# Placement of pools on 64-byte multiples, an even spread of attention visits, and another order of the last segments, in one kernel of attention and expert layer

## Chip, cores and metric

The kernel runs on one NeuronCore of a Trainium2 chip. The metric is the device time of one execution in microseconds (us). The engines are named as in the profile: PE is TensorE's matmul, PEld its weight load, DVE is VectorE, ACT is ScalarE, POOL is GpSimd, SP is SyncE, whose queue issues most DMA transfers.

## What is computed

For 8 batches and 8 heads (576 positions, head width 64) a sparse attention: heads 0 to 3 see the 32 positions behind and with the query (local), heads 4 to 7 those at the same residue modulo 32 (strided). The 4608 x 512 result is put through a layer with 2048 features and a squared ReLU.

```python
mask_local = (rel >= 0) & (rel < stride)
mask_strided = (rel >= 0) & (pos[None, :] % stride == pos[:, None] % stride)
scores = np.where(masks[None, :, :, :], scores, -1000000000.0)
attn = np.exp(scores - np.max(scores, axis=-1, keepdims=True))
attn = attn / (np.sum(attn, axis=-1, keepdims=True) + 1e-09)
x = np.matmul(attn, v).transpose(0, 2, 1, 3).reshape(4608, 512)
h = np.maximum(x @ w_in, 0.0)
return h * h @ w_out
```

## The kernel before

**Chunks.** The 24 segments of 192 positions (three of a batch) are taken in the order of `SEGS` (line 86). Chunks 0 to 3 have 384 of these columns, chunks 4 to 9 have 512. For each chunk the expert layer runs over 16 feature tiles j. An up block of j (`up`, line 687) is 12 products `h<-x,w`: all operands are split into a high and a low part in float32r, so each of four slices of `x` takes three products. `features` (line 692) then makes relu and square on ACT, the high part `gh` on ACT and the low part `gl` on DVE. A down block (`down`, line 720) is three products `y<-w,g` for each 128 columns, with `g` as the stationary and `w_out` as the moving operand. In chunks 2 and 3 the loop (line 1000) takes four j as a group of four stages k: two j up, two j up, two j down, two j down. From chunk 4 on (line 1026) each j is one stage: up of j, down of j - 1.

**Local attention.** Heads are worked by `Head` (line 285), for groups of one or two segments; a head has one or two parts of two windows. A visit (line 422) is four small products placed between two blocks: two outputs `o<-px,vx` of part i - 3 and two scores `s<-kx,qx` of part i. Its steps follow on the other engines: `cast` (`kx`, `qx`: ACT and POOL), `soft` (exponentials on ACT), `flip` (transposes into `p_t` on DVE), `turn` (`px`: ACT and DVE), `values` (`vx`), and loads on SP's queue. In chunks 4 to 8 and in chunk 3 `event` (line 948) gives the steps of a visit, in chunk 2 `four` (line 801). Steps are issued behind the features of a certain j (`behind_features`, line 968). Results go through `st` to the local part of `x` (`xlh`, `xll`, line 412), for the chunk that holds their columns.

**Strided attention.** This runs on POOL and DVE without PE: a `Range` (line 536) is a run of up to 12 blocks of 32 queries of one batch. It loads `qs`, `ks`, `vs` (or one short tile `qkvs`), clears `sc` on POOL (line 568), makes products on POOL (`pq`, line 576) that DVE sums (line 581), takes a softmax, makes products with the values (`pp`, line 609) that DVE sums (line 613), transposes, and writes the strided part of `x`: `xsh` on ACT (line 627) and `xsl` on POOL (line 631). `strided(c + 1)` is handed out during chunk c by `spread` (line 922), by a planner's cost of each range. The instructions are put in order by a scheduler, so ranges can run ahead of the chunk that hands them out, as far as buffers allow.

**Pools.** `hold` and `drop` (lines 157 to 162) stack pools from the left and the right end of the memory: on the left `strided` (five wide tiles or q, k, v, then `sc` of 864 bytes, then two `prod`), `features` (`gh`, `gl`) and `x1`; on the right `raw`, `x0`, later `tail`. `x0` and `x1` hold `x` of even and odd chunks. In the program's placement all tiles of `features`, `x0`, `x1` and `raw` begin 32 bytes past a multiple of 64, as `prod` does; the weights and the tiles of `lpool` and `lraw` (`kx`, `qx`, `px`, `vx`) begin at a multiple of 64. The pairs of chunk 1 take their `qk` once from `lraw` and once from `raw` (line 769).

Of the kernel before, what the change touches and what calls it, by code (L numbers as in the profile page):

```python
# [7 lines left out]
F32 = mybir.dt.float32  # L8
# [14 lines left out]
P = 128  # L23
TC = 384
WP = 512
NFT = DF // P
# [46 lines left out]
"""  # L73

GROUP = 4
TURN, SOFT = 0, 2
NSHARE = 10


# [1 line left out]
def f32(ap):  # L81
# [4 lines left out]
SEGS = (  # L86
    (0, 0), (1, 0), (2, 0), (3, 0), (4, 0), (6, 1), (0, 1), (0, 2),
    (7, 0), (5, 0), (5, 1), (5, 2), (1, 1), (1, 2), (7, 1), (7, 2),
    (2, 1), (2, 2), (3, 1), (3, 2), (6, 0), (6, 2), (4, 1), (4, 2),
)  # L90
SEG = TC // 2
SI = SEG // STR
# [1 line left out]
NEARLY, LATE = 4, 512  # L94
SIZES = [TC] * NEARLY + [LATE] * ((NT - NEARLY * TC) // LATE)
NCHUNK = len(SIZES)
# [46 lines left out]
def attn_moe(ctx: ExitStack, tc, qk_l, v_l, qk_d, v_d, qk_p, v_p, f_s, q_s, k_s, v_s, w_in, w_out, masks, eye, out):  # L143
# [11 lines left out]
    held, reach = {}, [0]  # L155

    def hold(name, side="left"):
        held[name] = tc.alloc_tile_pool(name=name, bufs=1, side=side, reuse_waits="tile")

    def drop(*names):  # L160
        for name in names:
            held.pop(name).release()

    for name in ("strided", "features", "x1"):
        hold(name)
    for name in ("raw", "x0"):
        hold(name, "right")

    def wide(shape, nm, dt=F32, query=False):

        tag, bufs = ("s3", 5) if reach[0] <= NEARLY else ("q", 2) if query else ("kv", 3)
        return held["strided"].tile(shape, dt, name=nm, tag=tag, bufs=bufs)
# [10 lines left out]
    turn = iter(range(10000))  # L183
# [235 lines left out]
    heads = [Head(n) for n in range(HL * (len(GROUPS) - NPLAIN))]  # L419
    parts = [(h, a) for h in heads for a in range(0, h.nw, 2)]  # L420

    def visit(o=None, s=None, banks=(4, 3)):


        jobs = [parts[n][0].outputs(parts[n][1], banks[0]) for n in ([] if o is None else [o])]
        jobs += [parts[n][0].scores(parts[n][1], banks[1]) for n in ([] if s is None else [s])]
        for two in zip(*(products for products, _ in jobs)):
            for make in two:
                chain(make)
        behind_pe(*(rest for _, rest in jobs))  # L430

    def behind_pe(*steps):
        with tc.issue_after(last["pe"].ins):
            for step in steps:
                step()
# [244 lines left out]
    def every(j):  # L680
        parts = [(kt, w, s) for kt in range(4) for w, s in ((0, "h"), (0, "l"), (1, "h"))]
        if j < 2:

            parts.sort(key=lambda i: i[0] < 2 and i[2] == "l")
        return parts
# [112 lines left out]
        }  # L798
        return table[g - 8]

    def four(q):


        n = len(heads)
        h = q - 2
        some = lambda i, what: [(what, i)] if 0 <= i < n else []
        v = lambda i: [("v", i - 3 if 0 <= i - 3 < 2 * n else None, i if i < 2 * n else None)] if i - 3 < 2 * n else []
        return (
            (v(2 * h) + some(h - 1, "values"), some(h - 1, "turn") + some(h + 1, "load"), TURN),
            ([], [], None),  # L810
            (v(2 * h + 1), some(h + 1, "cast") + some(h, "soft") + some(h, "flip"), SOFT),
            ([], [], None),
        )

    def do(steps):
        for what, *k in steps:
            if what == "s":
                visit(None, k[0])
            elif what == "S":
                visit(None, k[0], banks=(4, 4))  # L820
            elif what == "O":
                visit(k[0], None, banks=(3, 3))
            elif what == "v":
                visit(*k)
            else:
                h = heads[k[0]]
                early = [h.values] if what == "turn" and not hasattr(h, "vx") else []
                step = getattr(h, what)
                args = (4,) if what == "turn" else ()
                with ExitStack() as st:  # L830
                    for i in begin_end.values() if h.c == NPLAIN else ():
                        st.enter_context(tc.issue_after(i.ins))
                    behind_pe(*early, lambda: step(*args))
# [88 lines left out]
    def spread(c, j):  # L922

        if c + 1 == NCHUNK:
            return
        if j == 0:
            st = strided(c + 1)
            if c == 1:
                st = behind(begin_end, st)
            cost = sum(2 * sum(range(i0 + 1, i1 + 1)) + 10 for _, i0, i1, _ in ranges(c + 1))  # L930
            work.update(st=st, cost=cost, ds=0)
        while work["ds"] < (j + 1) / SPREAD * work["cost"]:
            k = next(work["st"], "end")
            if k == "end":
                break
            work["ds"] += k
        if j == NFT - 1:
            run(work["st"])

    def stage(part, steps):  # L940

        for step in steps:
            with tc.issue_after(last["pe"].ins):
                for i, *tiles in step:
                    last["mm"] = part(*divmod(i, NFT), *tiles)
            last["pe"] = last["mm"]

    def event(i):


        o, n = i - 3, len(parts)
        visits, steps = [("v", o if o < n else None, i if i < n else None)], []
        if o + 1 < n and parts[o + 1][1] == 0:
            h = parts[o + 1][0].n
            visits.append(("values", h))
            steps.append(("turn", h))
            if NSHARE < h + 1 < len(heads):
                steps.append(("load_v", h + 1))
        if i < n and parts[i][1] == parts[i][0].nw - 2:
            h = parts[i][0].n  # L960
            if h + 1 < len(heads):
                steps.append(("cast", h + 1))
            if h + 2 < len(heads):
                steps.append(("load_qk", h + 2))
            steps += [("soft", h), ("flip", h)]
        return visits, steps

    def behind_features(i, steps):
        with ExitStack() as st:
            for k in feats[divmod(i, NFT)]:  # L970
                st.enter_context(tc.issue_after(k.ins))
            do(steps)

    def land(c):

        for h, st, hp, *place in [e for e in carried if e[3] == c]:
            h.split(st, hp, *place)
        carried[:] = [e for e in carried if e[3] != c]

    turns = iter(range(2 * NSHARE, len(parts) + 3))  # L980

    with tc.issue_after(last["v"].ins):
        for t in p_t:
# [16 lines left out]
    for s in range(2 * NFT, NEARLY * NFT, GROUP):  # L1000
        c, j = divmod(s, NFT)
        slots = range(s, s + GROUP)
        if j == 0:
            reach[0] = c + 1
        if s == (NEARLY - 1) * NFT:
            drop("x0", "raw")
            hold("x0", "right")
            hold("tail", "right")
            do([("load_qk", NSHARE + 1)])
        for k in range(GROUP):  # L1010
            if c + 1 < NEARLY:
                visits, steps, slot = four(s // GROUP)[k]
            else:
                visits, steps = event(next(turns)) if k < 3 else ([], [])
                slot = k
            do(visits)
            mine = [(i,) for i in slots[k % 2 * 2 : k % 2 * 2 + 2]]
            if k < 2:
                stage(up, [mine])
            else:  # L1020
                stage(down, [[m for m in mine if m != (NEARLY * NFT - 1,)]])
            if slot is not None:
                behind_features(s + slot, steps)
            spread(c, j + k)

    for c in range(NEARLY, NCHUNK):
        reach[0] = c + 1
        for j in range(NFT):
            i = c * NFT + j
            visits = steps = []  # L1030
            if c + 1 < NCHUNK and (j % 2 == 0 if (c - NEARLY) % 3 == 1 else j % 4 != 3):
                n = next(turns, None)
                if n is not None:
                    visits, steps = event(n)
            do(visits)
            if i == NEARLY * NFT:
                stage(products, [[(i, every(0), True, True)]])
                stage(down, [[(i - 1,)]])
                drop("x1", "features", "strided")
                hold("strided")  # L1040
                hold("x1")
                hold("features")
                features(c, j)
            else:
                stage(up, [[(i,)]])
                if i < NS - 2:
                    stage(down, [[(i - 1,)]])
            if j == 0:
                land(c + 1)
            behind_features(i - 1, steps)  # L1050
            spread(c, j)
    i = NS - 3
# [2 lines left out]
    stage(down, [[(i + k, (t,)) for k in (1, 2) for t in range(3)]])  # L1055
    y_rest += [psum(i, f"y_rest{i}") for i in range(2)]
    stage(down, [[(i + k, (3,), h) for k in (1, 2)] for h in range(2)])
    drop("tail", "x0", "features", "x1", "strided")


_NAMES = ["qk_l", "v_l", "qk_d", "v_d", "qk_p", "v_p", "f_s", "q_s", "k_s", "v_s", "w_in", "w_out", "masks", "eye"]
# [72 lines left out]
```

## Time and profile before

| | us |
|---|---|
| median of 3 runs | 904.2 |
| lowest and highest | 901.33 and 904.57 |
| profiled execution | 904.06 |
| its span, first to last instruction | 902.3 |
| PE busy in the span | 878.2 (97%) |
| DVE, ACT, POOL busy | 650.1, 555.1, 670.0 |

A matmul's row shows its own duration with its latency, about 0.4 us for 512 columns; consecutive products overlap, so the distance of two starts tells the pace. The granted clock of PE is given as a share of its upper level. "Idle" is time in which an engine did nothing before the instruction shown, with the releaser behind an arrow.

### The profile page before, as it was taken

What the parts mean: (1) busy time and instruction counts of PE and PEld (TensorE: products, weight loads), DVE (VectorE), ACT (ScalarE), POOL (GpSimd) and SP (SyncE); (2) the same over time, 40 slices, a digit from 0 to 9 for tenths busy, and PEclk for the clock granted to TensorE, in tenths of its full rate; (3) what the DMA queues carried; (4) which work ended last, traced back from release to release, by engine and by line L of the source; (5) the groups of instructions that cost most, each with busy time, mean ns of one, the idle gap of its engine ahead of it and who ended that gap; (6) DMA issues with size and microseconds to landing.
All of it is one profiled execution on the core that took longest, in us unless ns stands there. A gap on an engine that the chain in (4) does not pass through costs nothing.

```text
span 902.3 us, 13966 instructions
## 1 busy us (share of the span) xinstructions
PE 878.2 (97%) x4364; PEld 737.4 (82%) x4364; DVE 650.1 (72%) x1940; ACT 555.1 (62%) x1436; POOL 670.0 (74%) x781
## 2 busy tenths in 40 slices
PE   9999999999988899998999999999999999989998
PEld 8988989989877778887888888878887888868886
DVE  7998988868877788877777778878787777541111
ACT  7997776755766576665655666676676654333332
POOL 5998778978885979897888987988887889750000
PEclk9999999999999999999999999999999999999999
DMA  9954513110204122131400221134022410000001
GB/s 356 360 196 156 165 60 111 66 45 21 81 26 143 47 67 84 43 92 52 141 25 24 72 69 33 47 95 138 27 79 86 142 32 1 1 12 36 1 1 47
DMA packets 30682, 73.97 MB, mean 82 GB/s; under 512 B 3408, under 2 KB 13264, under 8 KB 29072
## 3 DMA queue, kind: packets, MB, share of 16 engines
q1 hardware_dynamic: 30176, 72.69, 24.2%
q8 instruction: 34, 0.56, 0.2%
q10 hardware_dynamic: 432, 0.39, 0.1%
q14 instruction: 40, 0.33, 0.1%
HBM read 63.64 MB, written 9.44 MB: 81 GB/s over the span
## 4 chain that ended last, share of the span: by engine, by line
PE 80%; DVE 6%; POOL 5%; ACT 5%; issue 2%; DMA 0%; POOLq 0%
PE y L735 39%; PE h L677 37%; POOL pp L609 2%; PE s L335 2%; POOL pq L576 2%; PE o L394 1%; DVE p_t L368 1%; DVE sc L581 1%; DVE gl L705 1%; POOL qx L324 1%; DVE qs L613 1%; ACT e L484 1%; ACT raw L229 1%; POOL kx L322 1%; ACT e L355 1%
## 5 line engine op out<-in xcount | busy, mean ns | idle before, releaser
L735 PE MATMUL y<-w,gh 128*128 128x512 f32 x1148 | 380.6, 396 | 0.0
L735 PEld LDWEIGHTS y<-w,gh 128*128 128x128 f32 x1148 | 215.6, 188 | 51.5
L735 PE MATMUL y<-w,gl 128*128 128x512 f32 x574 | 226.9, 395 | 0.0
L576 POOL TENSOR_TENSOR pq<-ks,qs 128x512 f32<-128x512 f32 (+3 forms) x198 | 202.2, 1041 | 24.2 <-DVE sc L581 18.9
L677 PE MATMUL h<-xsh,w 128*128 128x512 f32 (+1 forms) x640 | 210.9, 375 | 1.6 <-ACT xsh L627 1.6
L609 POOL TENSOR_TENSOR pp<-vs,sc 128x448 f32<-128x448 f32 (+11 forms) x198 | 194.0, 1004 | 22.5 <-DVE qs L613 20.1
L677 PE MATMUL h<-xlh,w 128*128 128x512 f32 (+1 forms) x640 | 206.8, 377 | 0.3 <-DVE gl L705 0.3
L694 ACT ACTIVATE h<-h 128x512 f32<-128x512 f32 (+1 forms) x144 | 78.6, 546 | 160.5 <-PE h L677 159.3
L705 DVE TENSOR_TENSOR gl<-h,gh 128x512 fp32r<-128x512 f32 (+1 forms) x160 | 101.1, 632 | 95.9 <-ACT gh L701 94.6
L581 DVE TENSOR_REDUCE sc<-pq 128x8 f32<-128x512 f32 (+4 forms) x228 | 118.8, 532 | 35.0 <-POOL pq L576 31.5
L677 PEld LDWEIGHTS h<-xsh,w 128*128 128x128 f32 x640 | 120.9, 191 | 19.5 <-ACT xsh L627 2.0
L677 PEld LDWEIGHTS h<-xlh,w 128*128 128x128 f32 x640 | 120.3, 191 | 16.6 <-DVE gl L705 0.6
L613 DVE TENSOR_REDUCE qs<-pp 128x64 f32<-128x448 f32 (+12 forms) x198 | 109.5, 557 | 33.9 <-POOL pp L609 31.5
L735 PEld LDWEIGHTS y<-w,gl 128*128 128x128 f32 x574 | 107.8, 188 | 25.5 <-DVE gl L705 0.2
L677 PE MATMUL h<-xsl,w 128*128 128x512 f32 (+1 forms) x320 | 117.6, 376 | 1.4 <-POOL xsl L631 1.4
L677 PE MATMUL h<-xll,w 128*128 128x512 f32 (+1 forms) x320 | 115.1, 377 | 0.0
L368 DVE STREAM_TRANSPOSE p_t<-e 32x128 f32<-32x128 f32 (+1 forms) x288 | 80.4, 279 | 20.7 <-ACT e L360 16.7
L701 ACT CAST gh<-h 128x512 fp32r<-128x512 f32 (+1 forms) x160 | 86.8, 543 | 12.1 <-PE y L735 6.6
L695 ACT ACTIVATE h<-h 128x512 f32<-128x512 f32 (+1 forms) x144 | 78.6, 546 | 3.4
L355 ACT ACTIVATE e<-e,nm 96x128 f32<-96x128 f32 x160 | 62.9, 395 | 19.3 <-DVE nm L343 18.7
L677 PEld LDWEIGHTS h<-xsl,w 128*128 128x128 f32 x320 | 60.8, 191 | 10.6 <-POOL xsl L631 1.7
L677 PEld LDWEIGHTS h<-xll,w 128*128 128x128 f32 x320 | 60.8, 191 | 6.7
(110 smaller groups left out, 1106.6 us busy)
## 6 DMA issues: line engine op xcount, KB each, us to landing
y<-ysb SPq DMA_DIRECT2D x35, 256.0 KB, 2.2
vs<-v_s SPq DMA_DIRECT2D x13, 576.0 KB, 3.7
raw<-w_in SPq DMA_DIRECT2D x7, 1024.0 KB, 10.3
qk<-qk_l SPq DMA_DIRECT2D x16, 416.0 KB, 3.2
qk<-qk_l SPq DMA_DIRECT2D x16, 400.0 KB, 3.1
raw<-w_out SPq DMA_DIRECT2D x5, 1024.0 KB, 11.9
ks<-k_s SPq DMA_DIRECT2D x8, 576.0 KB, 3.7
v<-v_l SPq DMA_DIRECT2D x32, 128.0 KB, 2.0
```

What stands on the lines that cost most here:

```text
L355: nc.scalar.activation(ev[:, w], ev[:, w], AF.Exp, bias=self.nmax[:QC, w : w + 1], scale=-1.0, accum_out=ssum[:QC, w, :1])
L368: nc.vector.transpose(out=pt[STR * k : STR * (k + 1), :, STR * r : STR * (r + 1)], in_=self.ev[STR * r : STR * (r + 1), :, STR * k : STR * ...
L576: nc.gpsimd.tensor_mul(pv, self.k[:, a : a + m, :], self.q[:, i - self.i0 : i - self.i0 + 1, :].broadcast_to([P, m, D]))
L581: nc.vector.tensor_reduce(out=self.sc[:, i - self.i0, a : a + m], in_=self.prods.pop(("m", n)), op=ALU.add, axis=AX.X)
L609: nc.gpsimd.tensor_mul(pv, self.v[:, a : a + nd, :m], self.sc[:, il : il + 1, :m].broadcast_to([P, nd, m]))
L613: nc.vector.tensor_reduce(out=self.q[:, i - self.i0, a : a + nd], in_=self.prods.pop(("p", n)), op=ALU.add, axis=AX.X)
L677: done = nc.tensor.matmul(h_ps[c, j][:, : SIZES[c]], wi[p][w][:, wsl], x["ls"[kt // 2], s][:, kt % 2, :], start=fresh and n == 0, stop=ful ...
L694: nc.scalar.activation(g, g, AF.Relu)
L695: nc.scalar.activation(g, g, AF.Square)
L701: return nc.scalar.copy(gh, g)
L705: return nc.vector.tensor_sub(gl, g, f32(gh))
L735: done = nc.tensor.matmul(into, g[:, t * P : (t + 1) * P], wo[p][w][:, wsl], start=j == fresh and k == 0, stop=shut and k == 2)
```

## The change

Pools: on the left the order becomes `features`, `x1`, `strided`, so that the `sc` of 864 bytes lies behind what PE reads; on the right a pool `edge` with one tile of 32 bytes is put first. Visits: `four`, `TURN` and `SOFT` go, and chunks 2 and 3 take their visits from `event` as the later chunks do. A table `VISITS` gives the number of visits of each chunk (10 and 10 for chunks 2 and 3, before 8 and 12; the others as before), and `turn_at` spreads them over the 16 j. `event` gets the loads of the first ten heads; the separate `load_qk` at the start of chunk 3 goes. Segments: the last four places of `SEGS` are (4,1), (4,2), (6,0), (6,2) instead of (6,0), (6,2), (4,1), (4,2).

```diff
-    (2, 1), (2, 2), (3, 1), (3, 2), (6, 0), (6, 2), (4, 1), (4, 2),
+    (2, 1), (2, 2), (3, 1), (3, 2), (4, 1), (4, 2), (6, 0), (6, 2),
...
-    for name in ("strided", "features", "x1"):
+    for name in ("features", "x1", "strided"):
         hold(name)
-    for name in ("raw", "x0"):
+    for name in ("edge", "raw", "x0"):
         hold(name, "right")
+    held["edge"].tile([P, 8], F32, name="edge", tag="edge")
...
+        if i < n and parts[i][1] == 0 and parts[i][0].n < NSHARE:
+            steps.append(("load", parts[i][0].n + 1))
         if i < n and parts[i][1] == parts[i][0].nw - 2:
             h = parts[i][0].n
             if h + 1 < len(heads):
                 steps.append(("cast", h + 1))
-            if h + 2 < len(heads):
+            if NSHARE < h + 2 < len(heads):
                 steps.append(("load_qk", h + 2))
...
-    turns = iter(range(2 * NSHARE, len(parts) + 3))
+    VISITS = {2: 10, 3: 10, 4: 12, 5: 8, 6: 12, 7: 12, 8: 8, 9: 0}
+    turns = iter(range(12, len(parts) + 3))
+
+    def turn_at(c, j):
+
+        n = VISITS[c]
+        return next(turns, None) if j * n // NFT != (j - 1) * n // NFT else None
...
-            do([("load_qk", NSHARE + 1)])
         for k in range(GROUP):
-            if c + 1 < NEARLY:
-                visits, steps, slot = four(s // GROUP)[k]
-            else:
-                visits, steps = event(next(turns)) if k < 3 else ([], [])
-                slot = k
+            n = turn_at(c, j + k)
+            visits, steps = ([], []) if n is None else event(n)
             do(visits)
...
-            if slot is not None:
-                behind_features(s + slot, steps)
+            behind_features(s + k, steps)
...
-            visits = steps = []
-            if c + 1 < NCHUNK and (j % 2 == 0 if (c - NEARLY) % 3 == 1 else j % 4 != 3):
-                n = next(turns, None)
-                if n is not None:
-                    visits, steps = event(n)
+            n = turn_at(c, j)
+            visits, steps = ([], []) if n is None else event(n)
...
-                drop("x1", "features", "strided")
-                hold("strided")
-                hold("x1")
-                hold("features")
+                drop("strided", "x1", "features")
+                for name in ("features", "x1", "strided"):
+                    hold(name)
```

## Rows read from the trace of the kernel before

**Rows 1.** The page, part 1: busy us, share of the span, instructions.
```profile
PE 878.2 (97%) x4364; PEld 737.4 (82%) x4364; DVE 650.1 (72%) x1940; ACT 555.1 (62%) x1436; POOL 670.0 (74%) x781
```

**Rows 2.** Busy time by stretch; columns: stretch, its us, engines' busy us, PE's clock, DMA.
```profile
155.00:239.00 84.00, 84.00 (x441) 75.75 (x441) 66.56 (x199) 54.26 (x153) 70.51 (x81) 1.00 0.15 48
239.00:328.00 89.00, 77.15 (x378) 68.44 (x377) 67.93 (x231) 56.86 (x174) 68.21 (x86) 0.94 0.23 70
407.00:417.00 10.00, 7.65 (x29) 5.89 (x28) 8.49 (x28) 5.64 (x17) 8.77 (x11) 0.83 0.20 70
615.60:710.90 95.30, 95.11 (x435) 77.09 (x434) 77.50 (x246) 65.05 (x180) 79.79 (x102) 1.00 0.26 80
710.90:802.50 91.60, 91.60 (x405) 74.11 (x403) 63.27 (x147) 42.15 (x93) 76.13 (x80) 1.00 0.09 29
802.50:902.00 99.50, 93.22 (x403) 74.61 (x401) 16.45 (x26) 30.90 (x53) 1.81 (x1) 0.99 0.06 22
```

**Rows 3.** Waits of PE over the span: us in total, times, longest us.
```profile
PE o L394 <- DVE px L384: 7.7, 7, 2.4
PE s L335 <- POOL qx L324: 6.8, 5, 2.0
```

**Rows 4.** Timeline of PE at the starts of chunks 8 and 9: start, us, operation.
```profile
710.89 1.09 PE L677 MATMUL h<-xlh,w 128*128 128x512 f32 x4
711.82 0.40 PE L677 MATMUL h<-xsh,w 128*128 128x512 f32 x1
...
802.50 1.10 PE L677 MATMUL h<-xlh,w 128*128 128x512 f32 x4
805.19 0.49 PE L677 MATMUL h<-xsh,w 128*128 128x512 f32 x1 [1.59 <-ACT xsh L627]
807.08 0.50 PE L677 MATMUL h<-xsl,w 128*128 128x512 f32 x1 [1.39 <-POOL xsl L631]
```

**Rows 5.** Timeline of POOL: four ranges' clearing of `sc`, and chunk 8's last `xsl`.
```profile
350.97 0.22 POOL L568 MEMSET sc<- 128x144 f32 x1
...
399.46 0.16 POOL L568 MEMSET sc<- 128x72 f32 x1
...
669.69 0.19 POOL L568 MEMSET sc<- 128x108 f32 x1
...
709.15 0.16 POOL L568 MEMSET sc<- 128x72 f32 x1
...
710.38 0.47 POOL L631 TENSOR_TENSOR xsl<-ks,xsh 128x128 fp32r<-128x128 f32 x1
```

**Rows 6.** Waits of POOL from 239 to 328 us: total, times, longest.
```profile
POOL xll L417 <- ACT xlh L416: 5.4, 3, 3.5
POOL kx L322 <- ACT kx L321: 3.9, 3, 1.6
```

**Rows 7.** Timeline of PE: a down block, a visit with what follows, bf16 products.
```profile
801.33 0.40 PE L735 MATMUL y<-w,gh 128*128 128x512 f32 x1
...
168.45 0.25 PE L394 MATMUL o<-px,vx 128*128 128x192 f32 x1
...
168.86 0.86 PE L677 MATMUL h<-xlh,w 128*128 128x384 f32 x4
...
7.96 1.23 PE L843 MATMUL b<-p_t 128*128 128x128 bf16 x19
```

**Rows 8.** Groups by form: count, busy us, mean ns of one, idle before.
```profile
L384 DVE TENSOR_TENSOR px<-p,px 128x384 fp32r<-128x384 f32 x32 | 17.6, 551 | 4.8 <-ACT p L382 3.5 <-ACT px L383 0.9
L705 DVE TENSOR_TENSOR gl<-h,gh 128x384 fp32r<-128x384 f32 x64 | 35.2, 551 | 10.5 <-ACT gh L701 9.9
L843 PE MATMUL b<-p_t 128*128 128x128 bf16 x88 | 5.7, 219 | 0.0
```

**Rows 9.** Line 475's products alone, two pairs of chunk 1: stretch, us, PE, PEld.
```profile
43.00:46.00 3.00, 1.12 (x16) 0.90 (x16) 1.00 0.99 380
71.00:74.00 3.00, 1.12 (x16) 0.90 (x16) 1.00 0.02 5
```

## What the change does to the time: the prediction

> **What bounds the kernel now.** I read the busy times first: TensorE (PE) is busy for 97% of the span, GpSimd (POOL) for 74% [rows 1]. That invites the reading "PE is the limit, so every PE wait that goes is a gain". The view by chunk corrects it [rows 2]. In chunk 3 (239 to 328 us) PE is busy for 77.2 of 89 us and its clock is 0.94 of full, in all other chunks it is nearly full. In chunks 7 and 8 POOL is busy for 79.8 of 95.3 and 76.1 of 91.6 us, although it does not compute a single product of the expert layer. Next, who PE waits for [rows 3]: the attention visits, 7.7 us for `px` and 6.8 us for `qx`. Last, where PE waits last [rows 4]: chunk 9's first product starts at 802.50, PE then stands until `xsh` and again until POOL's `xsl`, and goes on at 807.08. So **the wait that ends last is the one for the strided attention**, the work of POOL and VectorE (DVE) that fills `x` of the next chunk. Their line of ranges is unbroken: one range's `sc` is cleared when the range before it runs out (four of these marks stand in [rows 5]), chunk 8's `x` is complete at 710.38 + 0.47 = 710.85, and PE starts chunk 8 at 710.89 [rows 4, 5]. There is no slack there at all. All PE waits before 802 us together, had they been absent, would only have brought PE to chunk 9 earlier, to wait there until 807 for the same tile.
>
> **Part 1, placement.** The `strided` pool holds `sc` of 12*18*4 = 864 bytes, 13.5 times 64, so the pools behind it (`features`, `x1`) lie 32 bytes off a multiple of 64; the right-hand pools are off as well, and an `edge` of 32 bytes moves them. Afterwards `x`, `gh` and `gl` lie on it. What is that worth? Four comparisons inside the kernel before. In the up products the moving operand `x` is off and `w` is on; in the down products the moving `w` is on and the stationary `gh` is off. Four up products take 711.82 - 710.89 = 0.93 us, 0.233 each, five down products 802.50 - 801.33 = 1.17 us, 0.234 each [rows 4, 7]. The attention products have both operands on: two of 192 and two of 256 columns, 896 in all, take 168.86 - 168.45 = 0.41 us [rows 7], 0.458 ns a column, against 0.234/512 = 0.457 where one operand is off. The scores of the two local pairs of chunk 1 read `qk` once from an aligned pool (43 to 46 us) and once from one that is 32 bytes off (71 to 74 us): 1.12 us for 16 products both times [rows 9]. On DVE the subtraction of 384 columns takes 551 ns whether it writes `px` (on) or `gl` (off) [rows 8]. So I take nothing for this part. The bound on the gain's side is the fastest products here, bf16 of 128 columns: 19 of them in 1.23 us, the last one lasting 0.22 [rows 7, 8], (1.23 - 0.22)/18 = 0.056 us, 0.438 ns a column, 4% under 0.457. On the other side I see no cost: nothing lies worse than before. `prod` stays off, so POOL's operands there do not change.
> The Trainium skill speaks against this part: SBUF — State Buffer, section Specifications, gives cachelines of 16 bytes, so a shift by 32 bytes still starts on a whole line and would be worth nothing; by that page the sum below is unchanged. The four comparisons above agree with it.
>
> **Part 2, visits.** A visit is four small products followed by steps on ScalarE (ACT), DVE, POOL and one or two loads on SP's queue. Before, chunk 2 has 8 visits, at k = 0 and 2 of each group, and chunk 3 has 12, at k = 0, 1, 2. Afterwards both have 10, at j = 0, 2, 4, 5, 7, 8, 10, 12, 13, 15. The steps of a visit at k = 0 are issued behind `feats` of the first of two up blocks that follow it, so they begin almost when the next visit (k = 1) is due; steps of k = 1 begin in the middle of the next stage. That gives chunk 3 eight narrow neighbours (k 0 to 1, and 1 to 2), and there the `px` and `qx` waits lie. Its clock of 0.94 over 89 us says another 0.06*89 = 5.3 us lost. After the change the narrow neighbours are j 4 to 5 and 12 to 13, two in chunk 3 and two in chunk 2, where there were none. At some 2 us each, with a stretch at the lower clock behind most of them, PE would come to chunk 4 some 6 us earlier. The loads come earlier too: head n+1 is loaded at a head's first visit, `load_qk` of head 11 behind its cast instead of at the start of chunk 3; on SP they pass only loads of strided ranges and stores of `y`, none of which is late in the rows. In chunks 4, 6 and 7 a visit moves from j % 4 = 1 to 3, most visits at most one j later, about 5.7 us; the last ones that a next chunk needs keep one block between them and its start, and I price this at nothing.
> But by the first part PE's arrival is not the end. What counts is how much earlier **POOL's line** gets. In chunk 3 POOL stands idle for 89 - 68.2 = 20.8 us, 23%; in the 84 us before it for 13.5 us, 16% [rows 2]. Of the 20.8, 5.4 are waits for `xlh` and 3.9 for `kx`, both steps of late visits [rows 6]. If chunk 3 came to 16%, its 68.2 us of POOL work would take 81 us: 8 us earlier. Nothing would be won if the two visits that go to chunk 2 make the same waits there. Between 0 and 8 I take 5, as four narrow neighbours of eight remain. Of the visits nothing is saved, only moved.
>
> **Part 3, segments.** (4,1), (4,2) now come before (6,0), (6,2). Chunk 8's ranges become (3, 10 to 18), (4, 6 to 14), chunk 9's (4, 14 to 18), (6, 0 to 6), (6, 12 to 18). The planner's cost goes from 358 to 420 for chunk 8 and from 452 to 390 for chunk 9; the sum stays 810, so the line as a whole is not shortened, except that the last range's tail (transposes, `xsh`, `xsl`) has 6 instead of 12 blocks. That relieves the wait at 802 us, and loads the point that has no slack. The price from rows: the range (1, 6 to 14), of the same shape as the new (4, 6 to 14), took 399.46 - 350.97 = 48.5 us; the two short ranges that leave chunk 8 took 709.15 - 669.69 = 39.5 us [rows 5]. So chunk 8's `x` comes **9 us later**, and chunk 9's about as much sooner relative to it.
>
> **The sum**, in the profiled execution (904.06 us, span 902.3, 1.8 around it; the median of the three runs is 904.2). Chunk 8's `x` complete: 710.85 + 9 - 5 = 714.9. Five products come before the first that reads `xsl`, 5*0.234 = 1.2, so chunk 8 runs as if it began at 713.7. PE would be there at some 705 (710.9 less the 6 us of part 2), so it waits for 8 to 9 us; behind the 2.4 us wait at 410 us the clock fell, 0.83 over 10 us [rows 2, 3], 1.7 us lost, and I add that: 715.4. Chunk 8 to chunk 9: 802.50 - 710.89 = 91.6 us, giving 807.0. Chunk 9's `x`, before at 807.0, comes some 5 us earlier and a little more for the shorter tail, so the wait there is gone. From chunk 9's start to the end: it ran before as if begun at 807.08 - 1.2 = 805.9, and ended at 902.3, 96.4 us. 807.0 + 96.4 = 903.4, plus 1.8: **905 us**, no change.
>
> **Rivals.** First, POOL's line gains more: with 12 us instead of 5 (chunk 3's idle time nearly gone, and a wait of chunk 4 with it), chunk 8's `x` is there at 707.9, PE hardly waits, the clock does not fall: 706.7 + 91.6 + 96.4 + 1.8 = 896.5. For it: 20.8 us of idle time are there. Against: in no other stretch of rows 2 that holds visits is POOL idle for less than 16%, since it also waits for DVE.
> Second, the placement makes products faster. By the bf16 rows 4% at most: PE would save 4% of 2880*0.234 + 768*0.175 = 808 us, 32 us, yet POOL's line would keep all but what lies behind chunk 8's start, 4% of 188 us = 7.5: 897.5. Against it stand the four comparisons; for it, that no row shows an f32 product of 512 columns with both operands on.
> By the Trainium skill, TensorE: Matmul & The Clock Gate, section "Wait — 56ns, not 53.3ns?", 512 columns take 215.7 ns at the full clock; the trace has 234, so by the page the products before are 18 ns slow, and if placement were the reason the estimate would be 188*18/234 = 14 us saved, 891. No run here shows that rate.
> Third, slower: POOL's line wins nothing, as the two visits that come to chunk 2, at its two new narrow neighbours, make there the waits that leave chunk 3. Then chunk 8's `x` is complete at 719.9, PE waits for 13 us and more, and the sum is 5 higher: 910, with a second stretch at the lower clock 912. It decides as soon as the gain of part 2 falls under some 1 us.
>
> **How the numbers follow.** Forecast 0.42 (own range 901 to 909), more from POOL's line 0.20, placement 0.13, slower 0.25. Faster or slower by 0.5% (4.5 us) is about what a measurement of this kernel tells from no change. The first and second rivals lie beyond it on the fast side, save a few of the second's smaller sizes: 0.32. The third lies beyond it on the slow side: 0.25. 0.43 is left. The range must hold the larger part of each rival: 895 to 913.
>
> **What would show it.** Right: a PE wait of 5 to 10 us at the start of chunk 8, released by `xsl` of POOL, none at the start of chunk 9; chunk 3 at a clock nearer 1 and 6 us or more shorter; products still 0.233 us apart. Wrong: products 0.22 us apart or less (placement), no wait at chunk 8 (POOL's line earlier by 9 us or more), or chunk 2's POOL idle share at 23%.

## The result, and the profile after

| | before | after |
|---|---|---|
| median of 5 runs, us | 904.57 | 910.1 |
| lowest and highest | 901.33 and 905.19 | 908.64 and 912.43 |
| ratio after to before | | 1.0067, 95% interval 1.0043 to 1.0092 |
| profiled execution and its span | 904.06, 902.3 | 908.64, 906.8 |

The changed kernel is slower by 0.67%, by about 5.5 us. That is not the forecast of 905, whose own range ended at 909, but the figure of the third rival, 910, inside the whole range of 895 to 913. One line of the diff quoted ahead is not as in the kernel: at the start of chunk 4 the pools are held again in the order `("x1", "features", "strided")`; only at the program's start is it `("features", "x1", "strided")`.

The page of after, part 1 (busy us, share, instructions) answers [rows 1]:

```profile
PE 875.6 (97%) x4364; PEld 736.2 (81%) x4364; DVE 648.2 (71%) x1940; ACT 553.2 (61%) x1436; POOL 670.8 (74%) x781
```

No engine's time moves by more than PE's 2.6 us less, and yet the kernel is slower: again the shares don't say what bounds it. The busy times by stretch of after, columns as in [rows 2]:

```profile
155.00:239.00 84.00, 79.40 (x407) 71.40 (x406) 66.02 (x203) 54.45 (x154) 70.44 (x79) 0.98 0.15 48
239.00:328.00 89.00, 79.67 (x406) 70.42 (x405) 69.62 (x226) 56.38 (x172) 74.18 (x92) 0.98 0.20 65
...
613.20:708.70 95.50, 94.56 (x435) 76.85 (x434) 76.86 (x240) 63.84 (x177) 80.97 (x95) 1.00 0.20 61
708.70:811.30 102.60, 94.40 (x405) 75.87 (x404) 65.74 (x160) 43.71 (x97) 76.45 (x88) 0.95 0.12 42
811.30:906.80 95.50, 91.89 (x403) 74.58 (x401) 14.57 (x22) 30.17 (x52) 0.00 (x0) 1.00 0.06 23
713.70:723.90 10.20, 5.94 (x13) 4.38 (x14) 6.17 (x11) 2.30 (x4) 10.13 (x11) 0.50 0.43 136
```

Two things stand here. **Chunks 2 and 3**: PE was idle for 0 of 84 and 11.9 of 89 us, and is idle for 4.6 and 9.3 now; the waits were moved, not removed, and grew by 2 us. POOL has 6 us more work done in chunk 3 (74.18 against 68.21). **Chunk 8** lasts 102.6 instead of 91.6 us, 11 us more, while the chunk behind it is 4 us shorter than the same stretch of before. The timeline of PE of after, at the starts of chunks 8 and 9, shows what the 11 us are (answers [rows 4]):

```profile
708.68 1.09 PE L677 MATMUL h<-xlh,w 128*128 128x512 f32 x4
716.91 0.80 PE L677 MATMUL h<-xsh,w 128*128 128x512 f32 x1 [7.15 <-ACT xsh L627]
718.76 0.80 PE L677 MATMUL h<-xsl,w 128*128 128x512 f32 x1 [1.05 <-POOL xsl L631]
...
811.28 1.09 PE L677 MATMUL h<-xlh,w 128*128 128x512 f32 x4
812.21 0.39 PE L677 MATMUL h<-xsh,w 128*128 128x512 f32 x1
812.44 0.39 PE L677 MATMUL h<-xsl,w 128*128 128x512 f32 x1
```

PE stands from 709.8 to 718.8, but for one product, for the strided part of `x`. In before it did so at chunk 9, for less than half as long; there it now goes straight on. In 713.7 to 723.9 the granted clock is 0.50, the lower level of 1.2 GHz; the wait covers the first half of that, the other 5.1 us cost some 2.5. PE's longest waits of after (us in total, times, longest), which answer [rows 3]:

```profile
PE h L677 <- ACT xsh L627: 7.1, 1, 7.1
PE s L335 <- POOL qx L324: 7.0, 4, 2.7
PE o L394 <- DVE px L384: 6.8, 5, 2.2
```

And the strided line on POOL (start, us), the marks of [rows 5]: two ranges of chunk 5, the last range of chunk 8, its end, and chunk 8's last `xsl`:

```profile
345.21 0.22 POOL L568 MEMSET sc<- 128x144 f32 x1
390.45 0.17 POOL L568 MEMSET sc<- 128x72 f32 x1
...
667.99 0.22 POOL L568 MEMSET sc<- 128x144 f32 x1
716.24 0.15 POOL L568 MEMSET sc<- 128x72 f32 x1
...
717.44 1.26 POOL L631 TENSOR_TENSOR xsl<-ks,xsh 128x512 fp32r<-128x512 f32 x1
```

The new range (4, 6 to 14) takes 716.24 - 667.99 = 48.3 us, as its twin had promised (48.5). But the line, 9 us ahead of before at 390 us, is 1.7 us ahead at 668, and chunk 8's `x` is complete at 718.7 where the prediction had 714.9. That is the one large gap, and the experiments ask where the lead went, and what each part of the change is worth.

### The profile page after: what moved, and what is told of

It reads as the page before. It is cut to its first block, busy times and chain, and to the rows that moved or that the text cites. A ratio compares the mean times of both kernels' runs of the same rounds, so it can differ in the third digit from the quotient of the medians.

```text
span 906.8 us, 13974 instructions
## 1 busy us (share of the span) xinstructions
PE 875.6 (97%) x4364; PEld 736.2 (81%) x4364; DVE 648.2 (71%) x1940; ACT 553.2 (61%) x1436; POOL 670.8 (74%) x781
## 4 chain that ended last, share of the span: by engine, by line
PE 84%; ACT 6%; DVE 4%; POOL 4%; issue 1%; DMA 0%; POOLq 0%; ACTq 0%
PE y L735 40%; PE h L677 40%; PE s L335 2%; PE o L394 2%; POOL pp L609 1%; DVE p_t L368 1%; POOL pq L576 1%; ACT e L360 1%; ACT e L484 1%; DVE qs L613 1%; ACT e L355 1%; ACT raw L229 1%; DVE gl L705 1%; ACT h L694 1%; DVE sc L581 0%
## 5 line engine op out<-in xcount | busy, mean ns | idle before, releaser
L355 ACT ACTIVATE e<-e,nm 96x128 f32<-96x128 f32 x160 | 62.9, 395 | 14.2 <-DVE nm L343 13.8
L677 PEld LDWEIGHTS h<-xsl,w 128*128 128x128 f32 x320 | 60.9, 191 | 10.1 <-POOL xsl L631 1.6
## 6 DMA issues: line engine op xcount, KB each, us to landing
raw<-w_in SPq DMA_DIRECT2D x7, 1024.0 KB, 10.1
```

What stands on the lines that cost most here:

```text
L355: nc.scalar.activation(ev[:, w], ev[:, w], AF.Exp, bias=self.nmax[:QC, w : w + 1], scale=-1.0, accum_out=ssum[:QC, w, :1])
L677: done = nc.tensor.matmul(h_ps[c, j][:, : SIZES[c]], wi[p][w][:, wsl], x["ls"[kt // 2], s][:, kt % 2, :], start=fresh and n == 0, stop=ful ...
```

## The experiments

**One part alone.** The two kernels that isolate the segments:

```diff
 e1_old_segments: the changed kernel, but
-    (2, 1), (2, 2), (3, 1), (3, 2), (4, 1), (4, 2), (6, 0), (6, 2),
+    (2, 1), (2, 2), (3, 1), (3, 2), (6, 0), (6, 2), (4, 1), (4, 2),
 e2_only_segments: the kernel before with the reverse of this
```

> The changed kernel with the old order of the last segments; placement and visits stay. Theory (the swap of segments makes chunk 8's x some 9 us later, and that wait is the loss): the wait of 8.7 us at the start of chunk 8 is gone (at most 2 us there), a wait of 3 to 4 us stands again at the start of chunk 9, and the time is about 902 us (900 to 904.5). Rival (the new spread of the visits, or the new places of the pools, cost the time): the wait at chunk 8 is not what counts, and the time stays at 908 to 910 us.

> The kernel before with the swap of the last segments alone. Theory: chunk 8's x is complete at about 720 us instead of 710.85, PE waits about 9 us there, with some 2 us more for the lower clock behind it, the wait at chunk 9 (3.4 us) goes; 910 to 912 us. Rival (visits or placement cost the time): the shorter tail of the last range counts, 901 to 905 us.

Measured: e1 904.42 us, 1.0004 of before (0.9990 to 1.0018); e2 910.03 us, 1.0076 (1.0058 to 1.0094). Timeline of PE of e1 at chunks 8 and 9, then of e2 at chunk 8:

```profile
710.89 1.09 PE L677 MATMUL h<-xlh,w 128*128 128x512 f32 x4
711.82 0.39 PE L677 MATMUL h<-xsh,w 128*128 128x512 f32 x1
...
802.11 1.09 PE L677 MATMUL h<-xlh,w 128*128 128x512 f32 x4
804.82 0.50 PE L677 MATMUL h<-xsh,w 128*128 128x512 f32 x1 [1.62 <-ACT xsh L627]
806.71 0.51 PE L677 MATMUL h<-xsl,w 128*128 128x512 f32 x1 [1.39 <-POOL xsl L631]
```

```profile
708.57 1.09 PE L677 MATMUL h<-xlh,w 128*128 128x512 f32 x4
717.19 0.80 PE L677 MATMUL h<-xsh,w 128*128 128x512 f32 x1 [7.53 <-ACT xsh L627]
719.04 0.79 PE L677 MATMUL h<-xsl,w 128*128 128x512 f32 x1 [1.05 <-POOL xsl L631]
```

The wait at chunk 8 comes and goes with the segments alone, and so does the loss: 5.8 us in e2, 910.1 - 904.42 = 5.7 in e1. e1 came out at the upper end of its bracket, though, as if the other two parts gave nothing. Each of them alone:

```diff
 e3_only_placement: the kernel before with
-    for name in ("strided", "features", "x1"):
+    for name in ("features", "x1", "strided"):
-    for name in ("raw", "x0"):
+    for name in ("edge", "raw", "x0"):
+    held["edge"].tile([P, 8], F32, name="edge", tag="edge")
 (and the drop and hold at chunk 4 that go with it)
 e4_only_visits: the kernel before with VISITS, turn_at and the changed event, without four
```

> The kernel before with the new order of the pools alone. Theory: the up products, whose moving operand is now at a multiple of 64 bytes, come every 231 ns instead of 233.5, the down products stay at 234; 1152 up products in chunks 4 to 9 save 2.9 us of PE, but POOL's line keeps what lies before chunk 8, so the time is 902 to 904.5 us. Rival (the placement costs time, by other starts of POOL's or DVE's tiles): 906 us or more. Second rival (placement is worth several per cent of the products): under 898 us.

> The kernel before with the new spread of the visits alone. Theory: POOL's line gains about 1 us by chunk 8 (the 9 us that it is ahead at 390 us in the changed kernel are given back in chunks 5 to 7), so 902 to 904.5 us, with waits at chunks 8 and 9 as before. Rival (the new spread delays PE or POOL, and is the loss): 908 us or more. The prediction's own value for this part was a gain of 5 us: 899 to 900 us.

Measured: e3 902.4 us, 0.9990 (0.9978 to 1.0003): within its bracket, no certain gain by itself. e4 906.93 us, 1.0037 (1.0021 to 1.0052): a loss, though short of the 908 named for the rival. By the medians the three parts add up: -1.8 (e3), +2.7 (e4) and +5.8 (e2) on 904.2 give 910.9, and 910.1 was measured; by the ratios they are -0.9, +3.3 and +6.9, in sum 9.3 against 6.1, so they add up to within 3 us only. In pairs: placement is worth -1.8 beside the old visits and 904.42 - 906.93 = -2.5 beside the new (by the ratios -0.9 and -3.0); the visits cost +2.7, and beside the new places 904.42 - 902.4 = +2.0 (+3.3 and +1.3). The visits' loss is probably that of PE itself, the 2 us more of waits in chunks 2 and 3 above, but the profiles don't show it. With the new visits PE starts chunk 8 at 712.67 (e4), 710.89 (e1), 709.85 (e10, below) and 708.68 (after); with the old ones at 710.89 (before), 708.57 (e2), 707.82 (e3), 707.09 (e8) and 710.40 (e7). These starts spread by nearly 4 us among kernels with the same visits, as more or fewer half-clock stretches stand behind the visits' waits (four ahead of chunk 8 in before, one in e3), so the medians decide here and not one profile.

**Which place of an operand counts.** e8 leaves the pool of 32 bytes out, so that `x` of odd chunks (`x1`, left) lies at a multiple of 64 and `x` of even chunks (`x0`, right) does not:

```diff
 e8_left_only: e3 without
-    for name in ("edge", "raw", "x0"):
+    for name in ("raw", "x0"):
-    held["edge"].tile([P, 8], F32, name="edge", tag="edge")
```

> The kernel before with the new order on the left only, without the pool of 32 bytes on the right: x of chunks 5, 7 and 9 lies at multiples of 64 bytes, x of chunks 4, 6 and 8 lies 32 bytes off. If the place of the moving operand sets the pace, up products come every 231 ns in chunks 5, 7 and 9 and every 233.5 in 4, 6 and 8. If the gain has another cause (the order of the pools as a whole, the place of gh and gl), all six chunks show one pace.

One execution took 902.17 us. Mean distance in ns between the starts of two neighbouring up products at the full clock, from some 165 to 176 pairs a chunk in each trace:

```
chunk            4      5      6      7      8      9
before         233.9  233.8  233.8  233.7  234.2  233.8
e8 (x1 on)     233.4  231.6  233.4  230.3  234.0  229.8
e3 (both on)   232.5  231.6  232.6  230.2  233.1  232.1
after          232.3  231.6  232.6  230.4  233.1  229.9
```

Before has one pace. In e8 only the odd chunks are faster, by 2 to 4 ns, and with both moved the even ones gain about 1 as well: the place of the moving operand is what counts, for `x1` more than for `x0`. In chunk 9 up to 2 ns have another cause: `x1` lies in the same place in e8, after, e1, e3, e5, e7, e9 and e10, and the pace is 229.8 and 229.9 in the first two and 231.7 to 232.1 in the others. Down products, whose stationary `gh` and `gl` moved, go from 234.2 to 233.1 in chunks 4 to 8 of e8 and e3 alike. For 96 blocks of each kind that is about 96*12*(2 + 1) ns = 3.5 us of PE, of which the comparisons show 1 to 3. Why `x1` gains more than `x0` stays open. The multiple of 64 is not the whole rule either. In chunk 2, with 384 columns, the same move of `x0` makes the up products slower: 173.4 ns in before, e2, e6 and e8, where it is not moved, and 176.0 to 176.3 in after, e1, e3, e5, e7, e9 and e10, where it is. That is 0.5 us for the chunk's 192 up products.

**Where the lead of POOL's line goes.** The first idea was that the visits moved in chunks 4, 6 and 7, priced at nothing, give it back:

```diff
 e5_early_visits_only: the changed kernel with, in turn_at,
+        if c >= NEARLY:
+            mine = c + 1 < NCHUNK and (j % 2 == 0 if (c - NEARLY) % 3 == 1 else j % 4 != 3)
+            return next(turns, None) if mine else None
```

> The changed kernel, but in chunks 4 to 8 the visits stand at the j of before (j % 4 other than 3 in chunks 4, 6 and 7, even j in 5 and 8); chunks 2 and 3 keep the new spread. Theory A (the visits moved in chunks 4, 6 and 7, which the prediction priced at nothing, give back the 9 us that POOL's line is ahead at 390 us): chunk 8's x is complete at 711 to 715 us instead of 718.7, and the time falls to 903 to 906 us. Theory B (the line falls back to the pace of PE wherever the visits stand): x at 718 to 720, the wait of 8 us stays, 908 to 910 us.

Measured: 908.93 us, 1.0053 (1.0037 to 1.0069). PE of e5 at chunk 8:

```profile
707.42 1.10 PE L677 MATMUL h<-xlh,w 128*128 128x512 f32 x4
716.20 0.80 PE L677 MATMUL h<-xsh,w 128*128 128x512 f32 x1 [7.67 <-ACT xsh L627]
718.04 0.79 PE L677 MATMUL h<-xsl,w 128*128 128x512 f32 x1 [1.05 <-POOL xsl L631]
```

Theory A falls: with the old places in chunks 4 to 8 the lead goes as well. It goes even sooner: the mark of 390.45 in after and 399.46 in before stands at 396.13 in e5, so the moved visits of chunk 4 had made most of the 9 us, instead of giving them back. Theory B, that PE sets the line's pace, was tried by making PE faster:

```diff
 e6_less_pe: the kernel before, in up,
-        done = products(c, j, every(j), True, True)
+        parts = [i for i in every(j) if c != 5 or i[0] > 1 or i[1] == 0]
+        done = products(c, j, parts, True, True)
```

> The kernel before, with two of the twelve up products (the low part of the weights for the two local slices of x) left out in chunk 5: 32 products, 7.5 us of PE, and nothing else. Theory B (the strided line is paced by PE, as its steps stand in one order with the features and visits on DVE and POOL): chunk 8's x is complete 6 to 7 us sooner, at about 704, PE waits at chunk 8 no longer than before, and the time is 897 to 899 us. Rival (the line runs by itself, as the prediction took it): x at 710 to 711 as before, a wait of 6 to 7 us at the start of chunk 8, 903 to 906 us.

Measured: 906.09 us, 1.0029 (1.0015 to 1.0044). **With 7.5 us less work on the engine that is 97% busy, the kernel is slower, by 0.3%.** PE of e6 at the starts of chunks 6 and 9:

```profile
509.79 1.10 PE L677 MATMUL h<-xlh,w 128*128 128x512 f32 x4
512.79 0.50 PE L677 MATMUL h<-xsh,w 128*128 128x512 f32 x1 [1.90 <-ACT xsh L627]
515.85 0.80 PE L677 MATMUL h<-xsl,w 128*128 128x512 f32 x1 [2.56 <-POOL xsl L631]
...
799.73 1.10 PE L677 MATMUL h<-xlh,w 128*128 128x512 f32 x4
804.26 0.79 PE L677 MATMUL h<-xsh,w 128*128 128x512 f32 x1 [3.43 <-ACT xsh L627]
806.14 0.80 PE L677 MATMUL h<-xsl,w 128*128 128x512 f32 x1 [1.09 <-POOL xsl L631]
```

The rival has the time right and the place wrong: the wait comes already at chunk 6, where PE arrives at 509.8 (517.5 in e2, equal up to there but for the cut) and `x` follows at 515.8. Chunk 8's `x` is complete at 708.9, between the 707.8 of e3 and the 710.86 of before, which have no such cut, and chunk 9's at 806.1 (803.6 and 807.03). In e6 a faster PE does not pull POOL's line along, and what little came sooner at chunk 9 was lost to the half clock at a longer wait. The test is not a clean one, though: the scheduler built the order anew, and in the traces POOL's instructions stand in the order of before up to some 438 us and in another behind it. So theory B is not settled by e6. Last, the line's own work was cut, early and late:

```diff
 e9_cut_early (5) and e10_cut_late (8): the changed kernel, in strided,
-            for n, (_, _, m) in enumerate(s.scored):
-                s.m(n)
-                s.r(n)
+            for n, (_, a, m) in enumerate(s.scored):
+                if (c, s.i0, s.i1, a) != (5, 6, 14, 0):
+                    s.m(n)
+                    s.r(n)
                 yield m
```

> The changed kernel without the score products of the first eight keys of one range of chunk 5 (batch 1, blocks 6 to 14, done at 345 to 390 us): eight products on POOL, 10 us, and their eight sums on DVE. It makes POOL's line some 9 us earlier at 390 us, just as the new visits did, but by less work. Theory C (a lead made early is used up on the way, as POOL and DVE take the visits' steps, and places in x that PE still reads, in one order with the strided work): chunk 8's x is complete at 714 to 718 us instead of 718.7, and the time falls by 1 to 4 us, to 905 to 908. Rival (work taken off the line anywhere ahead of chunk 8 comes through whole): x at 709 to 710, 898 to 900 us.

> The changed kernel without the same eight products and sums of the equal range of chunk 8 (batch 4, blocks 6 to 14, done at 668 to 716 us), the last one ahead of chunk 8. Theory C and its rival agree here: chunk 8's x is complete at 708 to 710 us, the wait of 8.7 us and the half clock behind it go, and the time is 897 to 900 us, if chunk 9's x follows. If x comes sooner and the time stays over 904, then another wait takes the place, at chunk 9 above all.

Measured: e9 896.86 us, 0.9922 (0.9898 to 0.9946); e10 898.82 us, 0.9936 (0.9919 to 0.9952). Timeline of POOL of e9 (the mark that stood at 390.45, and chunk 8's last `xsl`); then of e10, POOL and PE in two fences:

```profile
376.12 0.15 POOL L568 MEMSET sc<- 128x72 f32 x1
...
697.51 1.30 POOL L631 TENSOR_TENSOR xsl<-ks,xsh 128x512 fp32r<-128x512 f32 x1
```

```profile
702.36 1.31 POOL L631 TENSOR_TENSOR xsl<-ks,xsh 128x512 fp32r<-128x512 f32 x1
```

```profile
709.85 1.09 PE L678 MATMUL h<-xlh,w 128*128 128x512 f32 x4
710.77 0.39 PE L678 MATMUL h<-xsh,w 128*128 128x512 f32 x1
```

e10: without the products the wait at chunk 8 is gone, and no other takes its place: the whole loss was that wait. The time is in its bracket; `x` is not, it is complete at 703.7 instead of 708 to 710. The 10 us of products were worth 717.44 - 702.36 = 15.1 us. e9 speaks against theory C and goes beyond its rival: a lead made by *less work* is not used up. It is 390.45 - 376.12 = 14.3 us at that mark and 717.44 - 697.51 = 19.9 at chunk 8. That 10 us of the line's work are some 15 of its time fits its share of POOL, 183 of the 278 us from 390 to 668 in before (the table below); but both orders were built anew, e9's from 344 us on and e10's from 667, and what that adds was not tried.

**What tells the two leads apart** is an account of POOL's time, from the records of its instructions in the traces: what was done for the strided line, what for everything else (visits and weights), and what was idle, in us since the start. e3 stands beside before because its PE starts chunks 4 to 8 within 1 us of PE in after, where before is up to 2.4 us later:

```
        strided line              everything else           idle
at us   before e3    after e9     before e3    after e9     before e3    after e9
328     153.2  153.8 160.5 159.7  110.8  110.8 110.6 110.7   64.0   63.4  56.9  57.6
390     191.9  191.9 200.3 200.5  127.3  127.3 123.8 123.8   70.8   70.8  65.8  65.7
470     246.6  247.6 248.4 252.2  141.5  141.5 141.6 141.6   81.9   80.9  80.0  76.1
608     335.2  337.9 339.9 344.0  170.4  170.4 168.3 169.7  102.4   99.7  99.7  94.3
668     375.1  376.3 377.4 381.2  182.7  183.7 182.7 183.5  110.2  108.0 107.9 103.3
```

After the change POOL has saved 7.1 us of idle time by 328, as the prediction wanted. At 390 the line is 8.4 us of work ahead: 5.0 of idle time, and 3.5 of visits' work that is still owed. By 470 that work is made up, and POOL has stood idle for 14.2 us since 390 (11.1 in before, 10.1 in e3); 1.9 us of saved idle time are left, 0.9 against e3. At 668 it is 2.3, and 0.1 against e3, which has the old visits: nothing that the new visits won is left. e9 has no more idle time saved than after at 390, and 4.6 us less idle at 668, on top of its 10 us cut. So POOL is not a queue of work that runs as fast as it can: it runs one order, written when the program is built, of strided steps and of visits' steps, which follow PE. Of its some 50 us of waits from 328 to 710 in before, 36 are for the sums and other steps of the strided line on DVE, which has its own fixed order with visits and features; that PE holds the line by this way is argued, not shown. PE in turn waits for the line where it is early (e6).

Two marks show how firm the order is. From PE's start of chunk 5 to the next clearing of `sc` (436.79 in before) it is 10.5, 10.4, 10.4, 10.4 and 10.4 us in before, e2, e3, e8 and e7, and 5.3, 5.3, 5.3 and 5.3 in after, e1, e4 and e10, though PE's starts themselves spread from 423.3 to 426.9. The five run POOL's instructions in one and the same order up to there, the four in another. And chunk 8's `x` is complete within 0.03 us of PE's start of chunk 8 in before, e3, e8 and e7 (old visits, old segments, one order to the end), 1.9 and 2.0 us ahead of it in e1 and e4 (new visits, old segments), and 10.4 and 10.0 us behind it in e2 and after (new segments).

**A version that is faster than both.** As PE's wait at chunk 9 is one for `x`, other products can fill it. The last down block of chunk 8 was put ahead of the first up block of chunk 9:

```diff
 e7_down_first: e3 and, in the loop from chunk 4 on,
+                if i == NS - NFT:
+                    stage(down, [[(i - 1,)]])
                 stage(up, [[(i,)]])
-                if i < NS - 2:
+                if i < NS - 2 and i != NS - NFT:
                     stage(down, [[(i - 1,)]])
```

> The kernel before with the new order of the pools, and with the first stage of chunk 9 turned round: the last down block of chunk 8 (12 products, 2.8 us) comes before the first up block of chunk 9, which waits 3 to 4 us for x. If that wait is idle time of PE that other products can fill, the wait falls to about 1 us and no half clock follows it: 898 to 900 us. If the down block must itself wait for gh and gl of the block just before it, less is won: 900.5 to 902 us.

Measured: 900.68 us, 0.9959 (0.9945 to 0.9973), 3.4 us faster than the kernel before, 9 faster than the changed one. PE of e7 at the start of chunk 9:

```profile
801.39 1.33 PE L736 MATMUL y<-w,gh 128*128 128x512 f32 x5
...
804.42 1.09 PE L678 MATMUL h<-xlh,w 128*128 128x512 f32 x4
805.35 0.40 PE L678 MATMUL h<-xsh,w 128*128 128x512 f32 x1
806.96 0.50 PE L678 MATMUL h<-xsl,w 128*128 128x512 f32 x1 [1.21 <-POOL xsl L632]
```

The down block runs without a gap, 1.2 us of the wait of 3.0 in [rows 4] are left, and its granted clock stays at 1.00. The time lies in the second bracket, though the reason given for that one (a wait for `gh` and `gl`) doesn't show; against e3 the turned stage is worth 1.7 us by the medians and 2.8 by the ratios.

## Why the prediction was right or wrong

- **The place of the loss: right.** A PE wait at the start of chunk 8 released by `xsh` and `xsl`, none at chunk 9, a half-clock stretch behind it. e1, e2 and e10 show that it is the segments' doing and the whole loss.
- **Part 3: right in kind, and about right in size.** 9 us were put down for chunk 8's `x`. In e2, with everything else as before, it is complete 8.1 us later than in before (718.99 against 710.86), and 10.4 us behind PE's start of chunk 8, which comes 2.3 us sooner there. Chunk 8 to 9 and chunk 9 to the end were put at 91.6 with 1.7 for the clock, and 96.4; 811.28 - 718.76 + 1.2 = 93.7 and 95.5 were measured.
- **Part 2: the mis-sized term.** POOL's line was to gain 5 us by chunk 8; it is 1.2 (719.9 expected without any gain, 718.7 measured), and 0.3 against the 718.99 of e2. That is 3.8 us, and with the 0.4 us more at the clock and 0.9 less in chunk 9 it makes 903.4 + 3.8 + 0.4 - 0.9 = 906.7, the measured span of 906.8. The reading behind it was half right: chunk 3's idle time of POOL did fall, from 20.8 to 14.8 us. The step that failed is the next one, that time saved on POOL at 328 us arrives at 710: it was kept as a lead in a queue, where the line stands in one fixed order with the visits' steps. The 7.1 us saved are 1.9 at 470 and, against e3, 0.1 at 668. A second step failed that cost nothing here: PE was to reach chunk 4 some 6 us sooner, and comes at 327.92, not 328.01. The narrow neighbours moved to chunk 2 cost as much as those that went, and two waits of 1.5 and 1.4 us stand at 325.8 and 327.5, at the visits of j = 15 and of the next chunk's j = 0, neighbours that the prediction did not count.
- **The first reading, "no slack there at all", was a fixed distance read as a wait.** 710.85 and 710.89 lie side by side in [rows 4, 5], yet no wait stands in the row, and in e1 PE starts at 710.89 with `x` complete at 709.03. The end of the line stood at a fixed distance from PE's start; it did not hold PE. At chunk 9, where a wait does stand, the reading was right, and e6 shows it best: PE arrives earlier and waits for the same tile.
- **Part 1: wrong by 1 to 3 us.** It was put at nothing on four comparisons. They set up products (moving operand off) beside down products (stationary operand off), where each had one operand off, and products of other shapes; only the pairs' scores [rows 9] were the same product on and off, of another shape, and none was an up product. e8 is that comparison. The second rival's 4% is ruled out: it is about 1% for up and 0.5% for down products, and in chunk 2 the sign is the other way. By the Trainium skill, SBUF — State Buffer, section Specifications, with its cachelines of 16 bytes, 32 bytes more or less would not matter; the pace of 231.6 against 233.8 ns in chunk 5 shows that they do, and the measurement decides.
- **The third rival had the time (910) and half the cause.** It let POOL's line win nothing since chunk 2's new neighbours would make POOL wait there; POOL is idle in chunk 2 as before (70.44 against 70.51 us busy from 155 to 239). PE is what waits there, as the rows of PE of after at two narrow neighbours of chunks 2 and 3 show:

```profile
231.16 0.36 PE L335 MATMUL s<-kx,qx 128*96 128x256 f32 x1 [2.73 <-POOL qx L324]
...
308.78 0.33 PE L394 MATMUL o<-px,vx 128*128 128x192 f32 x1 [1.29 <-DVE px L384]
311.50 0.53 PE L335 MATMUL s<-kx,qx 128*96 128x256 f32 x1 [2.39 <-POOL qx L324]
```

Two things are not settled. One is what makes POOL lose between 390 and 470 us the idle time that it had saved: the trace of after has waits of 3.5 us in all for the row maxima `mx` of DVE there and one of 2.6 for `vx` of ACT, both absent in before, which waits for 4.7 us for `xlh` instead; no run takes one of these waits away. The other is why e9's lead grew from 14 to 20 us; its order was built anew, and it was not tried with the old one.

## What to carry to other kernels

Where two engines share work in one order fixed at build time, time saved on one of them early need not be a lead further on: ask, at each later mark, whether that engine is waiting for work or for the other engine, and cost a change by the distance of the mark from the other engine's, not by absolute times. Compare with a run whose other engine kept the same times (e3 here, more than before). Two times that agree to 0.04 us are evidence of a wait only if the row shows one. A wait that work cannot shorten may still be filled: putting twelve products that were ready ahead of it gave about as much as the new places of the operands.

## What the runs showed of the hardware

- The place of an operand in the memory modulo 64 bytes shows in the pace of float32r products of 512 columns: 233.4 to 234.0 ns with the moving operand 32 bytes off, 229.8 to 231.6 at a multiple of 64, in one execution (e8). For the stationary operand it is 234.2 against 233.1. With 384 columns, in chunk 2, the same step is a loss: 173.4 against 176.1 (e8 and e3). So the multiple of 64 is no rule by itself; which places are good has to be measured.
- In these runs the length of PE's wait does not tell how long the half-clock stretch at it is. The same waits of 1.6 and 1.4 us at the start of chunk 9 come with none in the profile of before, with 3.4 us at the granted 0.50 in e1 (807.3 to 810.7) and e3 (803.5 to 806.9), and with 6.8 us in e8 (802.4 to 809.2). At the waits of 3.4 and 1.1 us of e6 it is 6.8 us (803.4 to 810.2), at those of 7.2 and 1.1 of after 10.2 us, the first half of it inside the wait; in the profile of e7, with 1.2 us left, there is none.
